# A fused gated-attention and MLP kernel on one core: a new order table of the same operations

## The chip, the cores and the metric

The kernel runs on one core of a Trainium2 chip. The metric is the device time of one execution in microseconds, the median of the runs. The engines of the core are TensorE (PE, with its weight loads as PEld), VectorE (DVE), ScalarE (ACT), GpSimd (POOL) and SyncE (SP, which here issues most of the DMAs).

## The reference

Per batch (4) and head (8), over 768 steps of width 48, a gated linear attention with a complex decay is computed; its real part goes through a layer norm, an MLP with a hidden width of 4 x 384, and a residual.

```python
mag = np.sqrt(a_re * a_re + a_im * a_im)
scale = np.minimum(mag, 0.999) / (mag + 1e-06)
a_re_n, a_im_n = (a_re * scale, a_im * scale)
for t in range(S):
    new_re = ar * S_re - ai * S_im
    new_im = ar * S_im + ai * S_re
    kv = np.einsum('bhd,bhe->bhde', k[:, :, t], v[:, :, t])
    S_re, S_im = (new_re + kv, new_im)
    y[:, :, t] = np.einsum('bhd,bhde->bhe', q[:, :, t], S_re)
...
xn = (x - mu) / np.sqrt(var + 1e-06) * g_ln
ch = np.maximum(xn @ w_ch1, 0.0) @ w_ch2
return (x + ch)
```

## The kernel before

The 4 x 768 steps are cut into 24 chunks n of 128 steps, two chunks making one of 12 pairs P (three pairs per batch). Every operation has a name: `kind.P.half.part` for work on a pair (pair 0 is cut into two halves of its heads, the others have half 0 alone), `kind.n` for work on a chunk, `mm1.P.group.part` and `mm2.n.part` for the MLP.

For a pair: `are` and `aim`, `q`, `k` and `vf` are the loads. ACT takes `ln` of a_re and its reciprocal `iv`; `r` = a_im/a_re, `r2` its square, `u` the log of 1 + r2, and DVE sums `l` and clamps it (`lc`): the log of the decay. A matmul with a triangular matrix (`dec`, L481) sums it along time, and ACT makes `e` and `en`, the exponential and its inverse. `th` is the arctangent of r, `ph` (L506, L514) sums it along time on PE with a carry `car` from the pair ahead, and `sin`, `cos` come from ACT (`abs` or the quarter turn `qt` prepares the cosine). `qe` and `ke` are q and k times the exponentials, `qs` and `ks` these times cosine and sine, stacked in one 128-row operand. `qs` and `ks` are transposed to `qsT` and `ksT`, by PE (`qT`, `kT`, L612) with a copy by ACT or DVE, or by a transposing DMA on SP (L617).

For a chunk: `am` (L635) is the 128 x 128 score of each head, `atm` its masked copy (DVE, PSUM to SBUF), `gm` (L663) and `G` the state that is carried on, `y` (L685, L688) the output, `x` its copy in SBUF, `bn` the statistics of the layer norm, `xtr` (L706) with `xT` the transposed x; `rstd` the inverse deviation. Per pair, `mm1` (L740, weights w1b, the gain and the mean folded in by `wp` and `wc`) makes the hidden layer in three groups, `relu` copies it (ACT or DVE), `mm2` (L772, weights w2b) is the second product, `oa` and `ot` scale it and add x, and `st` stores. `wl.0` to `wl.5` load the weights from POOL's own DMA queue; `warm` (L805) are matmuls without a use, put into PE's waits in the start; `tab` (L810) are loads of ACT's function table, one for logarithm and exponential and one for sine and arctangent.

What sets the order is a table written out in the code, `PLAN`. Each word is one operation: its name, the engine after the colon (P, A, V, G, S for PE, ACT, DVE, POOL, SP), the PSUM bank where it has one, and behind an @ another operation after whose last instruction it has to wait, although no data go between them. These waits are called turns: they keep a POOL operation behind a DVE operation, since the two engines share a port to SBUF. The words are emitted one after another, so each engine gets its instructions in the order of the table and runs them in that order. Tiles are rings of two to ten buffers (`RINGS`); an operation that writes a ring's buffer again has to stand behind the last reader of that buffer.

Of the kernel before, what the change touches and what calls it, by code (L numbers as in the profile page):

```python
# [39 lines left out]
aim.0.0:A are.0.0:S pickf:V tab.log.0:A ln.0.0:A iv.0.0:A are.1.0:S gln:S ue:G cmean:G uth:V r.0.0:V are.0.1:S one:G  # L40
r2.0.0:A u.0.0:A l.0.0:V ln.1.0:A aim.0.1:S ln.0.1:A q.0.1:S iv.0.1:A pick:G@r.0.0 lc.0.0:V warm.0:P0 warm.1:P0
warm.2:P0 warm.3:P0 warm.4:P0 warm.5:P0 warm.6:P0 warm.7:P0 warm.8:P0 warm.9:P0 warm.10:P0 warm.11:P0 warm.12:P0
warm.13:P0 warm.14:P0 warm.15:P0 warm.16:P0 warm.17:P0 warm.18:P0 warm.19:P0 warm.20:P0 warm.21:P0 warm.22:P0
# [4 lines left out]
warm.47:P0 warm.48:P0 warm.49:P0 warm.50:P0 warm.51:P0 warm.52:P0 warm.53:P0 dec.0.1:P2 aim.2.0:S en.0.0:A6 pad.qs.2:G
k.0.1:S wl.1:G@lc.1.0 en.0.1:A2 iv.2.0:A wl.0:G r.2.0:V warm.54:P0 warm.55:P0 warm.56:P0 warm.57:P0 warm.58:P0
warm.59:P0 warm.60:P0 dec.1.0:P4 e.1.0:A4 qrow:G@r.2.0 en.1.0:A4 k.0.0:S are.3.0:S pad.qs.1:G e.0.1:A2 r2.2.0:V  # L50
ke.0.0.0:V car0.0:G e.0.0:A6 qe.0.0.0:V u.2.0:A wgc:V warm.61:P0 warm.62:P0 warm.63:P0 warm.64:P0 warm.65:P0
# [18 lines left out]
ph.3.0:P0 atm.2:V4 car.3.0:V0 u.3.0:A xtr.3:P2 xT.3:V2 y.2:P6 x.2:A6 abs.3.0:V0 r.4.0:G mm1.0.2.0:P4 tab.trig.5:A  # L70
sin.3.0:A0 G.3:V7 xtr.2:P2 xT.2:V2 k.3.1:S are.6.0:S bn.2:V mm1.0.2.1:P4 mm1.1.1.0:P2 are.7.0:S mm1.1.2.1:P6
mm1.1.1.1:P2 bn.3:V cos.3.0:A relu.0.2:V4 bn.1:V pad.ks.2:G@ks.1.0.1 mm1.1.2.0:P6 relu.1.2:V6 mm1.1.0.1:P4 l.3.0:V
are.5.0:S ke.2.0.1:G@ks.1.0.1 ks.2.0.0:V th.4.0:A mm1.1.0.0:P4 mm2.0.0:P0 lc.3.0:V relu.1.1:A2 q.4.0:S qs.2.0.0:V
aim.6.0:S mm2.1.0:P3 mm2.1.1:P3 r2.4.0:G@ks.1.0.0 tab.log.6:A u.4.0:A ks.2.0.1:V vf.3.0:S aim.5.0:S relu.1.0:A4
# [137 lines left out]
def kernel(  # L212
# [13 lines left out]
    B, H, S, D = q.shape  # L226
# [615 lines left out]
```

## Time and profile before

| what | value |
|---|---|
| runs | 189.58, 189.34, 189.30 us; median 189.34 us |
| span of the profiled execution (first to last instruction) | 187.08 us, 2.26 us under the median of the runs |
| busy | PE 176.4, DVE 153.7, ACT 160.0, POOL 111.1 us |
| loads of ACT's table | 19, 24.4 us |
| HBM read, written | 28.31 MB, 4.72 MB |

The page gives a span for its execution, and no time of its own for it. Busy time of PE counts matmuls from issue to end, and consecutive ones overlap, so 176.4 us is more than the array needs. A row of the chain of waits or of the list in order of time begins with the start in us from the span's start and the duration in us. In the groups by line, the columns are line, engine, operation, tiles written and read with their shapes, count, busy us in all, mean ns of one, and the idle time ahead of them with what ended it.

### The profile page before, as it was taken

The page shows a single profiled execution, that of the slowest core. Times are in us where ns is not written, and L with a number is a line of the kernel's source. Part 1 is how long each engine was busy: PE and PEld are TensorE (multiplying, and loading weights), DVE is VectorE, ACT ScalarE, POOL GpSimd, SP SyncE. Part 2 cuts the span into 40 slices and gives each one's busy share as a digit, 9 for nine tenths or more (in the row PEclk, how much of TensorE's full clock was granted, in tenths as well). Part 3 has the DMA queues.
Part 4 walks back from the last instruction along what each step waited for, and adds up shares of the span by engine and source line. Part 5 has one row for each costly group of instructions (what it writes and reads, how often), then busy time and mean ns, then how long its engine had stood idle before and what let it go on. Part 6 is the DMA issues. An engine that isn't in the chain of part 4 may idle for free.

```text
span 187.1 us, 5110 instructions
## 1 busy us (share of the span) xinstructions
PE 176.4 (94%) x2025; PEld 135.1 (72%) x2027; DVE 153.7 (82%) x275; ACT 160.0 (86%) x228; POOL 111.1 (59%) x130
## 2 busy tenths in 40 slices
PE   5978898999999999999999999999999998999993
PEld 3756565787767789866687696878867866778772
DVE  1479999999989999999979989899879888866332
ACT  3889999999999989999999999998999897274560
POOL 3328699589207996288176692365879759420600
PEclk9999999999999999999999999999999999999999
DMA  5999999999999999699999997999999969996122
GB/s 148 291 256 227 223 260 189 207 206 194 233 261 239 219 221 191 128 203 309 204 155 238 256 265 92 185 247 169 216 175 215 203 144 229 210 199 173 40 90 84
DMA packets 132439, 37.39 MB, mean 200 GB/s; under 512 B 126528, under 2 KB 132416, under 8 KB 132416
## 3 DMA queue, kind: packets, MB, share of 16 engines
q1 hardware_dynamic: 123040, 32.45, 83.9%
q0 software_dynamic: 2784, 2.36, 8.2%
q10 hardware_dynamic: 6592, 2.26, 4.7%
q8 instruction: 16, 0.26, 0.6%
q14 instruction: 7, 0.06, 0.1%
HBM read 28.31 MB, written 4.72 MB: 177 GB/s over the span
## 4 chain that ended last, share of the span: by engine, by line
PE 71%; DVE 10%; DMA 6%; ACT 4%; POOL 3%; SPq 2%; issue 2%; DVEq 0%; POOLq 0%
PE banks L772 25%; PE banks L740 21%; PE banks L635 5%; PE banks L612 4%; PE banks L506 4%; PE banks L481 4%; DMA aim<-in_a_im_dram 3%; PE banks L685 2%; DMA qsT<-qs 2%; PE banks L706 2%; PE banks L688 2%; DMA are<-in_a_re_dram 2%; PE banks L663 2%; SPq L408 1%; DVE r L293 1%
## 5 line engine op out<-in xcount | busy, mean ns | idle before, releaser
L772 PE MATMUL banks<-w2b,h 128*128 128x384 bf16 (+1 forms) x300 | 53.8, 319 | 0.0
L740 PE MATMUL banks<-xT,w1b 128*128 128x256 bf16 x432 | 51.4, 272 | 0.2 <-DVE xT L290 0.2
L740 PEld LDWEIGHTS <-w1b 128*128 128x128 bf16 x432 | 41.3, 98 | 6.3 <-issue 0.4
L772 PEld LDWEIGHTS <-h 128*128 128x128 bf16 x300 | 27.1, 97 | 13.3
L293 DVE TENSOR_TENSOR atm<-banks,mask 128x1024 bf16<-128x1024 f32 x24 | 28.8, 1219 | 5.1 <-PE banks L635 5.0
L757 ACT ACTIVATE h<-banks 128x1024 bf16<-128x1024 f32 (+1 forms) x24 | 23.8, 1003 | 5.3 <-PE banks L740 5.1
L293 POOL TENSOR_TENSOR qe<-q,e 128x384 bf16<-128x384 f32 x19 | 17.5, 929 | 15.7 <-ACT e L485 9.1
L810 ACT ACT_TABLE_LOAD x19 | 24.4, 1283 | 1.7 <-PEq L826 1.3
L293 POOL TENSOR_TENSOR ke<-k,en 128x384 bf16<-128x384 f32 x16 | 14.8, 939 | 7.5 <-DVE qs L293 6.8
L759 DVE TENSOR_SCALAR h<-banks 128x1024 bf16<-128x1024 f32 (+1 forms) x13 | 15.2, 1169 | 3.6 <-PE banks L740 3.6
L805 PE MATMUL banks<-u_e 128*128 128x256 f16 x111 | 15.5, 297 | 2.2 <-POOL u_e L322 2.2
L635 PE MATMUL banks<-qsT,ksT 128*128 128x128 bf16 x192 | 14.1, 219 | 1.0 <-DMA qsT<-qs 0.7
L805 PEld LDWEIGHTS <-u_e 128*128 128x128 f16 x111 | 11.5, 106 | 4.5 <-POOL u_e L322 1.9
L293 POOL TENSOR_TENSOR r<-aim,are 128x768 f16<-128x768 f32 x7 | 12.6, 1811 | 3.0 <-ACT are L454 3.0
L635 PEld LDWEIGHTS <-ksT 128*128 128x128 bf16 x192 | 11.9, 98 | 2.5 <-issue 1.1
L293 POOL TENSOR_TENSOR qs<-qe,trig 128x768 bf16<-128x768 bf16 (+1 forms) x8 | 12.6, 1576 | 1.6 <-DVE qe L293 0.9
L470 DVE SCALAR_TENSOR_TENSOR l<-r,w 128x768 f16<-128x768 f16 (+1 forms) x13 | 12.3, 949 | 1.3 <-ACT r L466 1.1
L785 POOL TENSOR_TENSOR ot<-ot,x 128x384 f32<-128x384 f32 x11 | 10.5, 966 | 4.6 <-ACT ot L778 4.3
L698 DVE BATCH_NORM_STATS2 stats<-x 128x6 f32<-128x384 bf16 x24 | 13.1, 548 | 0.0
L288 ACT CAST x<-banks 128x384 bf16<-128x384 f32 x19 | 8.8, 478 | 5.0 <-PE banks L688 4.5
L293 POOL TENSOR_TENSOR ks<-ke,trig 128x768 bf16<-128x768 bf16 (+1 forms) x7 | 10.7, 1539 | 2.8 <-DVE qs L293 1.6
L685 PE MATMUL banks<-v,atm 128*128 128x48 bf16 x192 | 11.9, 183 | 0.0
(101 smaller groups left out, 380.4 us busy)
## 6 DMA issues: line engine op xcount, KB each, us to landing
q<-in_q_dram SPq DMA_DIRECT2D x24, 192.0 KB, 4.7
k<-in_k_dram SPq DMA_DIRECT2D x24, 192.0 KB, 4.5
are<-in_a_re_dram SPq DMA_DIRECT2D x11, 384.0 KB, 4.8
aim<-in_a_im_dram SPq DMA_DIRECT2D x11, 384.0 KB, 4.8
vf<-in_v_dram SPq DMA_DIRECT2D x19, 192.0 KB, 4.3
out_dram<-ot SPq DMA_DIRECT2D x18, 192.0 KB, 3.5
w1b<-in_moe_w_ch_dram POOLq DMA_DIRECT2D x3, 384.0 KB, 6.4
w2b<-in_moe_w_ch_dram POOLq DMA_DIRECT2D x3, 384.0 KB, 7.8
```

The source lines that it names most:

```text
L293: {"DVE": nc.vector, "POOL": nc.gpsimd}[eng(name)].tensor_tensor(**kw)
L470: nc.vector.scalar_tensor_tensor(out=S_("l"), in0=S_("r2"), scalar=0.5, in1=S_("w"), op0=ALU.mult, op1=ALU.add)
L635: nc.tensor.matmul(ps[:, h], lhsT=T("ksT", n)[:, h], rhs=T("qsT", n)[:, h], start=True, stop=True)
L685: nc.tensor.matmul(ps[:, h], lhsT=T("atm", n)[:, h], rhs=T("v", P)[:, c, h], start=True, stop=nfirst)
L698: nc.vector.bn_stats(out=T("stats", n), in_=T("x", n))
L740: nc.tensor.matmul(ps[:, jj], lhsT=w1b[:, dc, ts(gi * JG + jj, C)], rhs=T("xT", P)[:, dc].rearrange("p c t -> p (c t)"), start=(dc == 0), ...
L757: act(out=dst, in_=src, func=AF.Relu)
L759: nc.vector.tensor_scalar(out=dst, in0=src, scalar1=0.0, scalar2=None, op0=ALU.max)
L772: nc.tensor.matmul(bank(own)[:, 0:w], lhsT=T("h", P)[:, j, ts(c, C)], rhs=w2b[:, j, es], start=(j == 0), stop=(j == NJ - 1))
L785: nc.gpsimd.tensor_tensor(out=T("ot", n)[:, es], in0=T("ot", n)[:, es], in1=T("x", n)[:, es], op=ALU.add)
L805: g.add(f"warm.{i}", lambda i=i: nc.tensor.matmul(bank(f"warm.{i}")[:, 0:256], lhsT=u_e[:, 0, 0], rhs=u_e[:, 1].rearrange("p j t -> p (j t ...
L810: g.add(f"tab.{nm}.{i}", lambda tab=tab: nc.scalar.preload_act_table_set(tab))
```

## The change

`PLAN` is replaced by another table of the same operations; beside it, only the number of fillers that can be named is raised (111 to 200, of which the new table uses 103 where the old one used 111). Nothing of what an operation does is changed. The diff, of the table a line or two alone:

```diff
 PLAN = """
-aim.0.0:A are.0.0:S pickf:V tab.log.0:A ln.0.0:A iv.0.0:A are.1.0:S gln:S ue:G cmean:G uth:V r.0.0:V are.0.1:S one:G
...
+ue:G pad.qs.2:G car0.1:G are.0.0:S aim.0.0:S are.0.1:S tab.log.0:A car0.0:V are.1.0:S ln.0.0:A iv.0.0:A aim.0.1:S
...
-    for i in range(111):
+    for i in range(200):
         g.add(f"warm.{i}", lambda i=i: nc.tensor.matmul(
```

The table is two lines shorter, so every line number behind it is smaller by 2 in the new kernel. What the new table has otherwise than the old, counted by words (old, new):

| | old | new |
|---|---|---|
| turns (words with an @) | 49 | 35 |
| `warm` | 111 | 103 |
| `tab` | 19 | 18 |
| `qe` on POOL, on DVE | 19, 5 | 9, 15 |
| `ks` on POOL, on DVE | 7, 19 | 12, 14 |
| `r2` on ACT, POOL, DVE | 4, 4, 5 | 1, 7, 5 |
| `relu` on ACT, DVE | 24, 13 | 27, 10 |
| `v` on ACT, POOL, DVE | 2, 7, 3 | 4, 8, 0 |
| `vf` loads from ACT's queue, from SP's | 5, 19 | 0, 24 |
| `xT` by ACT, DVE, transposing DMA | 13, 10, 1 | 10, 12, 2 |

Three places show how the order moves. The first is DVE's queue at the end of the start, from the last products of the folded weights (L392, in the new kernel L390) to the masked scores and statistics of chunks 2, 3 and 0; the numbers in the names are buffers (atm2 is chunk 2's, sh1 is abs.3.0, car0 is written by car.3.0, xT1 by xT.3 and xT.2). Before:

```order
L392 SCALAR_TENSOR_TENSOR w1b_180<-w1b_180,gln_179,banks_63 128x512 x3
L293 TENSOR_TENSOR atm3_127<-banks_63,mask_174 128x1024
L290 CAST G2_130<-banks_63 128x384
L698 BN_STATS stats0_142<-x0_132 128x6
L699 BN_AGGR mv0_146<-stats0_142 128x2
L293 TENSOR_TENSOR atm2_126<-banks_63,mask_174 128x1024
L527 TENSOR_SCALAR car0_167<-banks_63 32x384
L290 COPY xT1_157<-banks_63 128x3x128
L551 TENSOR_REDUCE sh1_105<-banks_63 128x768
L293 TENSOR_TENSOR G3_131<-banks_63,dec1_95 128x384
L290 COPY xT1_157<-banks_63 128x3x128
```

Now:

```order
L390 SCALAR_TENSOR_TENSOR w1b_180<-w1b_180,gln_179,banks_63 128x512 x2
L291 TENSOR_TENSOR atm3_127<-banks_63,mask_174 128x1024
L390 SCALAR_TENSOR_TENSOR w1b_180<-w1b_180,gln_179,banks_63 128x512
L288 CAST G2_130<-banks_63 128x384
L291 TENSOR_TENSOR atm2_126<-banks_63,mask_174 128x1024
L696 BN_STATS stats0_142<-x0_132 128x6
L697 BN_AGGR mv0_146<-stats0_142 128x2
L549 TENSOR_REDUCE sh1_105<-banks_63 128x768
L288 COPY xT1_157<-banks_63 128x3x128 x2
L291 TENSOR_TENSOR G3_131<-banks_63,dec1_95 128x384
L525 TENSOR_SCALAR car0_167<-banks_63 32x384
```

The masked scores of chunk 2 (atm2) have moved ahead of chunk 0's statistics, one part of the folded weights behind atm3, and car0 and G3 behind both xT1 copies.

The second is SP's queue of loads in the start, behind the first loads of pair 0's k (k0_73); are0_64 is are.3.0, are1_65 is are.4.0, aim0_67 is aim.3.0, and q, k and vf carry their pair's number as the buffer's. Before:

```order
L449 DMA are0_64<-in_a_re_dram 128x8x96
L408 DMA k2_75<-in_k_dram 128x8x48
L408 DMA q1_71<-in_q_dram 128x8x48
L408 DMA q2_72<-in_q_dram 128x8x48
L408 DMA q1_71<-in_q_dram 128x8x48
L449 DMA are1_65<-in_a_re_dram 128x8x96
L408 DMA vf0_76<-in_v_dram 128x8x48
L408 DMA k1_74<-in_k_dram 128x8x48
L449 DMA aim0_67<-in_a_im_dram 128x8x96
L408 DMA k1_74<-in_k_dram 128x8x48
L408 DMA vf1_77<-in_v_dram 128x8x48
L408 DMA q2_72<-in_q_dram 128x8x48
```

Now:

```order
L370 DMA gln_179<-in_moe_g_ln_dram 128x3x1
L406 DMA q1_71<-in_q_dram 128x8x48 x2
L447 DMA are0_64<-in_a_re_dram 128x8x96
L406 DMA k1_74<-in_k_dram 128x8x48
L447 DMA aim0_67<-in_a_im_dram 128x8x96
L406 DMA vf0_76<-in_v_dram 128x8x48 x2
L406 DMA k1_74<-in_k_dram 128x8x48
L406 DMA q2_72<-in_q_dram 128x8x48
L406 DMA vf1_77<-in_v_dram 128x8x48 x2
L447 DMA are1_65<-in_a_re_dram 128x8x96
L406 DMA q2_72<-in_q_dram 128x8x48
L447 DMA aim1_68<-in_a_im_dram 128x8x96
```

The loads of q and k of pair 2 and of are.4.0 have moved behind those of k of pair 1, of aim.3.0 and of v of pair 0 (vf0); half of vf0 came from ACT's queue before and stands here now.

The third is SP's queue late in the program, at the transposes of chunks 20 and 21 (chunk 20 is buffer 0, chunk 21 buffer 1); xT1_157 is chunk 18's transposed x. Before:

```order
L712 DMA_TRANSPOSE xT1_157<-x8_140 128x3x128
L617 DMA_TRANSPOSE ksT1_117<-ks1_111 128x8x128
L408 DMA q2_72<-in_q_dram 128x8x48
L617 DMA_TRANSPOSE ksT0_116<-ks1_111 128x8x128
L617 DMA_TRANSPOSE qsT1_121<-qs1_114 128x8x128
L617 DMA_TRANSPOSE qsT0_120<-qs1_114 128x8x128
L408 DMA vf1_77<-in_v_dram 128x8x48 x2
```

Now:

```order
L710 DMA_TRANSPOSE xT1_157<-x8_140 128x3x128
L406 DMA q2_72<-in_q_dram 128x8x48
L406 DMA k2_75<-in_k_dram 128x8x48
L615 DMA_TRANSPOSE qsT1_121<-qs1_114 128x8x128
L615 DMA_TRANSPOSE ksT1_117<-ks1_111 128x8x128
L615 DMA_TRANSPOSE qsT0_120<-qs1_114 128x8x128
L615 DMA_TRANSPOSE ksT0_116<-ks1_111 128x8x128
L793 DMA out_0_dram<-ot4_166 128x384
```

The four transposes now stand in a row with the one for chunk 21's q first, its k second, and both loads of pair 11 ahead of them; a store follows where the loads of v did.

More of the change, by code (lines that the diff above doesn't have):

```diff
@@ L70 @@
[L70 to L74, printed above, removed]
```

195 lines of the change are left out of this document (99 added, 96 removed).

## The prediction

> **What bounds the kernel now.** The stretches come first: a table of busy time, cut at the two moments that the chain of waits marks (45.07, where it turns to matmuls, and 183.90, where the last matmul is over).
>
> ```profile
> core 0: us, PE busy (x) PEld busy (x) DVE busy (x) ACT busy (x) POOL busy (x), PEclk, DMA share, GB/s
> 7.86:45.07 37.21, 32.85 (x389) 25.02 (x391) 33.55 (x62) 35.76 (x52) 27.30 (x39) 1.00 1.16 226
> 45.07:183.90 138.83, 137.92 (x1604) 105.94 (x1603) 117.76 (x207) 119.90 (x171) 80.50 (x78) 1.00 0.95 195
> 183.90:187.08 3.18, 0.00 (x0) 0.00 (x0) 0.42 (x1) 0.00 (x0) 0.00 (x0) 1.00 0.28 90
> ```
>
> From 45.07 to 183.90 TensorE is busy 137.92 of 138.83 us at the full granted clock (1.00), while DVE is at 85% and ACT at 86%. A busy PE is not a PE at its peak, so the next view is its rows in order of time: in the chain of waits they follow each other at the rate of their size.
>
> ```profile
> 45.07 4.09 PE banks L740 x36
> 80.20 2.60 PE banks L772 x16
> 164.12 0.34 PE banks L706 x6
> 154.88 4.00 DMA qsT<-qs
> 179.96 3.94 PE banks L772 x36
> 183.93 0.42 DVE ot L788
> ```
>
> 36 matmuls of 256 columns in 4.09 us are 0.11 us each, 16 of 384 columns in 2.60 us are 0.16 us each. From 45.07 on nothing but such rows stands in the chain, apart from one piece around 154.88. So the kernel is three pieces: a filling of 45.07 us, 138.8 us of matmuls end to end, and 3.2 us behind the last of them (one DVE operation and the last store). An operation that goes from one other engine to another inside the middle piece is worth nothing unless a matmul waits for it. What can move the end: the moment at which the dense piece starts, the holes in it, and its amount of matmuls.
>
> **The dense piece starts when DVE lets it.** DVE in order of time, then ACT and PE at that place:
>
> ```profile
> 40.56 0.55 DVE L698 BATCH_NORM_STATS2 stats<-x 128x6 f32<-128x384 bf16 x1
> 41.15 0.18 DVE L699 BATCH_NORM_AGGREGATE mv<-stats 128x2 f32<-128x6 f32 x1
> 41.25 1.19 DVE L293 TENSOR_TENSOR atm<-banks,mask 128x1024 bf16<-128x1024 f32 x1
> 42.47 0.56 DVE L527 TENSOR_SCALAR car<-banks 32x384 f16<-32x384 int16 x1
> 43.07 0.36 DVE L290 COPY xT<-banks 128x384 bf16<-128x384 bf16 x1
> 43.34 0.95 DVE L551 TENSOR_REDUCE sh<-banks 128x768 f16<-128x768 int16 x1
> 44.21 0.55 DVE L293 TENSOR_TENSOR G<-banks,dec 128x384 bf16<-128x384 f32 x1
> 44.67 0.35 DVE L290 COPY xT<-banks 128x384 bf16<-128x384 bf16 x1
> 43.33 0.48 ACT L288 CAST x<-banks 128x384 bf16<-128x384 f32 x1
> 43.86 0.34 PE L706 MATMUL banks<-ident,x 128*128 128x128 bf16 x3
> 45.07 1.14 PE L740 MATMUL banks<-xT,w1b 128*128 128x256 bf16 x9 [0.21 <-DVE xT L290]
> ```
>
> The row at 45.07 is the first matmul of pair 1's hidden layer, and it waits for the second xT copy (44.67, chunk 2). That copy's input, the transpose at 43.86, was over at 44.20; the copy came 0.5 us later because abs (43.34) and G.3 (44.21) stood ahead of it.
>
> **Change, part 1: the start.** The operations of PE ahead of that matmul are the same ones in both tables, in another order, so the moment can be compared directly. In the new DVE order atm.2 stands ahead of chunk 0's statistics, and car.3.0 and G.3 stand behind the two xT copies. By start-to-start spacings of the rows: old, from 40.56: statistics 0.69, atm 1.22, car 0.60, xT.3 0.27, abs 0.87, G.3 0.46, xT.2 0.35, which ends at 45.02. New, from the same moment: atm.2 1.22, statistics 0.69, abs 0.87, xT.3 0.27, xT.2 0.35, which ends at 43.96. The difference is car and G.3: 0.60 + 0.46 = **1.06 us**. PE and ACT allow it: atm.2 would end 0.69 earlier, so y.2, x.2 and the transpose (1.42 us from atm's end at 42.44 to the transpose's start at 43.86) are ready from 43.17, ahead of where DVE would take the copy. What becomes late next is G.3, which feeds G's chain and no matmul of the next microseconds (gm.4 stands 16 us of PE work further on in the new order), and car.3.0, read by the phase of pair 4, 13 us on.
>
> Upstream of 40.56 more moves. Two half-width squares go from ACT to DVE, where a full-width product of 2-byte operands takes 0.55 us (the ks row of part 3), and the exponentials of half 0 are taken ahead of ln.2.0. The load queue is put in the order of need:
>
> ```profile
> 13.33 3.67 SPq L408 DMA_DIRECT2D q<-in_q_dram  x3
> 17.10 4.20 SPq L449 DMA_DIRECT2D are<-in_a_re_dram  x1
> 21.34 1.44 SPq L408 DMA_DIRECT2D vf<-in_v_dram  x1
> 22.82 0.77 SPq L408 DMA_DIRECT2D k<-in_k_dram  x1
> ```
>
> In the old table one are load holds the SP queue for 4.20 us (others take about 1), and v and k of the first pairs stand behind it. In the new one, q.2 and k.2 and that are load go behind k.1, aim.3 and vf.0. DVE had no long idle from 20 to 40 in the old run (9.52 and 9.44 busy of 10, below), so earlier data can bring only what DVE is relieved of; and the products of the first pairs that change between DVE and POOL nearly cancel (two qe and the two squares come to DVE, two ke, one qs and one ks leave it).
>
> ```profile
> 20.00:30.00 10.00, 9.07 (x90) 5.79 (x90) 9.52 (x20) 9.57 (x16) 8.51 (x11) 1.00 1.15 236
> 30.00:40.00 10.00, 9.06 (x136) 7.59 (x136) 9.44 (x15) 9.89 (x13) 8.12 (x9) 1.00 1.09 201
> ```
>
> DVE's idle in these 20 us is 1.04 us in all: the gain upstream is at most that, and at worst a loss of the same size (a new wait where an idle one was). I take 0.2 us of gain, since DVE gets no more work there than it loses and its inputs come earlier. Start: **-1.26 us**, between -2.1 and 0.
>
> **Part 2: the hole.** In the dense piece, the one wait of PE that the table of waits shows is for a transposing DMA:
>
> ```profile
> 151.31 1.23 SPq L617 DMA_TRANSPOSE ksT<-ks  x1
> 152.60 0.57 SPq L408 DMA_DIRECT2D q<-in_q_dram  x1
> 153.27 1.43 SPq L617 DMA_TRANSPOSE ksT<-ks  x1
> 154.88 3.19 SPq L617 DMA_TRANSPOSE qsT<-qs  x2
> 159.01 0.61 PE L635 MATMUL banks<-qsT,ksT 128*128 128x128 bf16 x8 [0.71 <-DMA qsT<-qs]
> ```
>
> am.21 waits 0.71 us for qsT.21, third in a row of four transposes. In the new order qsT.21 is the first of the four and ksT.21 the second, with two small loads ahead of both; that takes one transpose issue (1.43) and its spacing off am.21's wait and adds one load (0.57): about 0.9 us earlier, enough for 0.71. What is late next: am.20, which needs the fourth transpose; in the new PE order a block of mm2.19 (0.65) lies between the two. I take -0.5 of the 0.71 (0 to -0.71).
>
> **Part 3: amounts.** xtr.22 leaves PE (chunk 22 goes through a DMA transpose instead): three transposes, half of the six in 0.34 us, **-0.17 us**. It costs if the transposed x.22 comes later than mm1.11; it is put behind two stores on SP, with some 4 us of PE work between y.22 and mm1.11 as cover. Another table load goes from ACT, and products change between DVE and POOL:
>
> ```profile
> L810 ACT ACT_TABLE_LOAD x19 | 24.4, 1283 | 1.7 <-PEq L826 1.3
> L293 POOL TENSOR_TENSOR qe<-q,e 128x384 bf16<-128x384 f32 x19 | 17.5, 929 | 15.7 <-ACT e L485 9.1 <-DVE r L293 4.1 <-DVE qs L293 1.4
> L293 POOL TENSOR_TENSOR ks<-ke,trig 128x768 bf16<-128x768 bf16 x6 | 9.7, 1636 | 2.7 <-DVE qs L293 1.6 <-DVE ke L293 1.0
> L293 DVE TENSOR_TENSOR qe<-q,e 128x384 bf16<-128x384 f32 x5 | 2.7, 554 | 0.8 <-ACT e L485 0.8
> L293 DVE TENSOR_TENSOR ks<-ke,trig 128x768 bf16<-128x768 bf16 x16 | 8.6, 550 | 0.2
> ```
>
> The table load (1.28 us) is the last one, at a place where the matmuls hide ACT; ten qe go to DVE (+5.5 us there, -9.3 on POOL), five ks to POOL (-2.8 and +8.2). Three relus and three v copies leave DVE as well, so that neither DVE nor ACT ends with more work than before. All this lies beside 138.8 us of matmuls: 0, and with that cover gone it would show as the port rival below. Eight fillers fewer of 0.11 us each fill waits in the start: 0. The small other holes of the dense piece (0.91 - 0.71 = 0.2 us by the busy sum) I leave as they are. The tail has the same form, one DVE operation and a store: 0.
>
> Sum: -1.26 - 0.5 - 0.17 = **-1.9 us**: a span of 187.08 - 1.9 = 185.2. The median of the runs, 189.34, lies 2.26 above the span; with that kept, **187.4 us**.
>
> **Rivals.**
> 1. *The port takes it back (slower).* An unguarded POOL operation beside a DVE one holds it up:
>
> ```profile
> 17.70 0.91 POOL L293 TENSOR_TENSOR qe<-q,e 128x384 bf16<-128x384 f32 x1 [0.56 <-ACT r L466]
> 17.82 1.20 DVE L293 TENSOR_TENSOR ke<-k,en 128x384 bf16<-128x384 f32 x1
> ```
>
> The ke product took 1.20 us where its like took 0.55, and ended 0.41 us after POOL's end, so it stood still meanwhile: 0.65 us. The new table has 35 turns (waits that keep POOL behind a DVE operation) where the old has 49, and puts more of the long ks (1.64 us) on POOL; a DVE product that starts just behind a ks could stand up to 1.6 us. It decides where DVE feeds a matmul at once. From three such places of 0.65 us the gain is gone; with five the kernel is at 187.4 + 3.2 = 190.6 us. For it: fewer turns, more POOL work. Against it: DVE's 21 us of idle in the dense piece, and less DVE work. The Trainium skill (SBUF — State Buffer, Who interferes with whom) says that the pair of ports is an exclusive lock and that the second to start is blocked wholly; the two rows agree with it. By that rule alone, with every lost turn (14) costing DVE as in that row, 9 us would be added to DVE, still inside its 21 us of idle.
> 2. *No gain at the start (about the same).* Another input sets 45.07: the new order needs v, k, xT and weights in other places, and a weight load at a bad moment stops SP as the 4.20 us row does. Then only 0.17 and part of the hole remain: 189.1 us, and with a wait of 0.3 us more, no change.
> 3. *The upstream gain arrives too (faster).* -2.1 at the start, all of 0.71, 0.17 and 0.2 of the small holes: 186.2 us.
> 4. *The change is in name only:* the table load and the fillers are gone by count (19 to 18, 111 to 103), but neither is on the path, and were the order neutral elsewhere, 189.2. It is part of case 2.
>
> **How the numbers follow.** My forecast (186.7 to 188.5) 0.54; case 3 0.14; cases 2 and 4 0.15 (0.09 within 0.2%, 0.05 faster, 0.01 slower); case 1 0.17. The range reaches from case 3's 186.2, a little lower for its own spread, to near the middle of case 1: 186.0 to 190.0. The smallest change that can be told here is about 0.2%, 0.4 us. Faster: 0.54 + 0.14 + 0.05 = 0.73; within 0.2%: 0.09; slower: 0.17 + 0.01 = 0.18.
>
> **What would show it.** In the changed profile the first matmul of pair 1's hidden layer starts near 43.8; PE has no wait for a transposing DMA near 157; the last matmul ends near 182.0; the dense piece is 138.1 us long. Part 1 is wrong if that matmul starts after 44.7, part 2 if PE still waits over 0.5 us for ksT or qsT. The port rival shows as DVE products of 0.9 us and more where 0.55 is normal, with PE waits for DVE behind them. A dense piece longer than 140 us would make the prediction wrong whatever the start does.

## The result, and the profile after

After: 196.47 us, median of 4 runs (195.79 to 198.06); before, in the same session, 189.46 (189.30 to 190.81). Ratio 1.034, 95% interval 1.027 to 1.041: the new order is **slower by 3.4%**, 7.0 us, where 1.9 us of gain was forecast. Some executions fall into a slower state, and every ratio here is of the others alone, while the medians are of all (sp_later, fill, back6, y18, p1 and actq_late below have one or two slow ones).

The profiled execution has a span of 195.9 us (before 187.1); it is the slowest of the four, with a mean granted clock of 0.983, where the fastest, 195.79 us, had 1.000 and the other two 0.991. The table of busy time, cut as in the prediction (first decay matmul, first matmul of pair 1's hidden layer, end of the last matmul):

```profile
core 0: us, PE busy (x) PEld busy (x) DVE busy (x) ACT busy (x) POOL busy (x), PEclk, DMA share, GB/s
8.96:47.46 38.50, 34.25 (x383) 25.68 (x385) 33.00 (x59) 33.16 (x49) 22.98 (x28) 0.91 1.06 208
47.46:192.72 145.26, 138.56 (x1603) 105.50 (x1600) 120.45 (x212) 121.94 (x166) 85.94 (x82) 1.00 0.93 187
```

The start is 47.46 and not 45.07 (+2.4), the middle piece 145.26 and not 138.83 (+6.4), with nearly the same busy time of TensorE in it (138.56, before 137.92): mostly holes, then (6.7 us, before 0.9). The tail (192.72 to 195.90) is the same 3.18. And a column that was 1.00 throughout before: the granted clock of the start is 0.91.

**The start.** The changed kernel's rows in order of time (start, duration, engine; in brackets the idle time before and what ended it):

```profile
20.07 2.03 DVE L377 TENSOR_SCALAR gc<-cmean,gln 128x128 bf16<-128x128 f32 x3
...
20.24 1.78 POOL L291 TENSOR_TENSOR qs<-qe,trig 128x384 bf16<-128x384 bf16 x2 [0.87 <-ACT trig L530]
...
22.16 0.39 PE L386 MATMUL banks<-w1b,gc 128*128 128x512 bf16 x1 [1.35 <-DVE gc L377]
```

wgc, three small operations on DVE, takes 2.03 us beside two POOL products that nothing holds back (qs.0.0.1, qs.0.1.1); wp.1 on TensorE waits 1.35 us for it, and the carry car.0.1 behind it on DVE holds the next matmul for 0.74 us. TensorE is then sparsely busy, and this follows (busy time by stretch, the granted clock third from the end):

```profile
20.00:23.00 3.00, 0.98 (x4) 0.40 (x5) 2.94 (x7) 1.77 (x4) 1.78 (x2) 0.94 1.23 232
23.00:26.00 3.00, 2.72 (x10) 0.97 (x10) 2.97 (x7) 0.86 (x2) 1.04 (x2) 0.50 0.86 202
26.00:29.00 3.00, 3.00 (x12) 1.67 (x11) 0.95 (x2) 2.97 (x4) 3.00 (x4) 0.50 1.00 194
```

TensorE was busy for 0.98 of 3.00 us, and for the next six it was granted half its clock: 10 and 12 matmuls where the rows of before have 24 and 37. The Trainium skill (TensorE: Matmul & The Clock Gate, Part 1: The HAM clock gate) says that the clock halves after an idle window of about 3.4 us and that the windows run free of the program; the trace agrees with the halving, though TensorE was sparse there and not idle.

**The middle piece.** What TensorE waits for in it, from the table of waits (window 47.46 to 193):

```profile
PE banks L633 <- DMA ksT<-ks: 2.0, 1, 2.0
PE banks L479 <- DVE h L757: 1.6, 1, 1.6
PE banks L738 <- DVE qsT L288: 0.9, 1, 0.9
PE banks L633 <- DMA qsT<-qs: 0.8, 1, 0.8
```

With three smaller ones (0.6 for ACT's e, 0.3 for the transposing DMA of an xT, 0.2 for DVE's atm) these make 6.4 us, 3.1 of it for transposing DMAs. The same table of before, from 45.07 to 184, has 0.7 us for such a DMA and 0.2 for DVE. Two of the holes show what is new. At l.3.0 (behind it on DVE stands relu.1.2, which frees the bank of the matmuls dec.3.0):

```profile
49.49 0.80 POOL L368 DMA_DIRECT2D w2b<-in_moe_w_ch_dram  x1
49.64 2.43 DVE L468 SCALAR_TENSOR_TENSOR l<-r,w 128x768 f16<-128x768 f16 x1
50.32 0.93 POOL L291 TENSOR_TENSOR ke<-k,en 128x384 bf16<-128x384 f32 x1
...
54.46 0.81 PE L479 MATMUL banks<-l,u_e 128*128 128x384 f16 x4 [1.61 <-DVE h L757]
```

l.3.0 took 2.43 us (0.95 in before): it stood through POOL's descriptor writing for wl.5 and through the product behind it. The largest hole is at am.20 (chunk 20's scores), 1.97 us at 170.16. The chain of waits leads there:

```profile
147.03 2.65 DMA out_dram<-ot
149.78 0.62 DVE ot L786
...
152.79 1.64 POOL qs L291
154.43 1.43 issue
155.90 0.91 POOL ke L291
156.89 3.56 POOL ks L291 x2
...
163.94 1.33 SPq L615
165.31 4.80 DMA ksT<-ks
170.16 0.62 PE banks L633 x8
```

It runs through SP's queue, through a store on which DVE's ot.15 waits, through POOL's products and into the fourth of four transposing DMAs. (The 1.43 us of "issue" ahead of ke.10.0.1 end as its load k.10.1, issued at 152.66, lands at 155.83.) And SP itself had stopped long before. Its longest wait but the one for the last outputs, from the table of waits:

```profile
SPq L615 <- POOL ks L291: 8.0, 1, 8.0
```

8.0 us in one piece, 71 to 79, ahead of the transposing DMA ksT.8, whose input ks.4.0.1 had moved to POOL. No load left in that time.

### The profile page after: what moved, and what is told of

The parts are those of the page before. It is cut to its first block, busy times and chain, and to the rows that moved or that the text cites. A ratio compares the mean times of both kernels' runs of the same rounds, so it can differ in the third digit from the quotient of the medians.

```text
span 195.9 us, 5097 instructions
## 1 busy us (share of the span) xinstructions
PE 177.9 (91%) x2014; PEld 135.0 (69%) x2016; DVE 156.3 (80%) x277; ACT 160.3 (82%) x221; POOL 115.3 (59%) x133
## 4 chain that ended last, share of the span: by engine, by line
PE 32%; DVE 24%; DMA 11%; SPq 11%; ACT 8%; issue 6%; POOL 6%; POOLq 0%; DVEq 0%; ACTq 0%
PE banks L738 10%; PE banks L770 9%; SPq L406 5%; DMA out_dram<-ot 4%; DVE atm L291 4%; DVE l L468 3%; DMA aim<-in_a_im_dram 3%; SPq L447 3%; SPq L615 3%; PE banks L504 2%; DMA ksT<-ks 2%; DMA are<-in_a_re_dram 2%; DVE h L757 2%; PE banks L633 2%; POOL ks L291 2%
## 5 line engine op out<-in xcount | busy, mean ns | idle before, releaser
L770 PE MATMUL banks<-w2b,h 128*128 128x384 bf16 (+1 forms) x300 | 54.5, 319 | 0.0
L755 ACT ACTIVATE h<-banks 128x1024 bf16<-128x1024 f32 (+1 forms) x27 | 26.7, 1005 | 6.7 <-PE banks L738 6.5
L291 POOL TENSOR_TENSOR ks<-ke,trig 128x768 bf16<-128x768 bf16 (+1 forms) x12 | 18.4, 1545 | 4.4 <-DVE ks L291 2.9
L291 POOL TENSOR_TENSOR qs<-qe,trig 128x768 bf16<-128x768 bf16 (+1 forms) x9 | 13.2, 1476 | 7.3 <-DVE qe L291 4.1
L416 POOL TENSOR_SCALAR v<-vf 128x768 bf16<-128x768 f32 x8 | 7.2, 899 | 17.0 <-DVE qsT L288 7.7
L291 POOL TENSOR_TENSOR r<-aim,are 128x768 f16<-128x768 f32 x6 | 11.2, 1866 | 6.7 <-ACT are L452 6.7
L468 DVE SCALAR_TENSOR_TENSOR l<-r,w 128x768 f16<-128x768 f16 (+1 forms) x13 | 13.4, 1030 | 1.6 <-ACT r L464 1.6
L757 DVE TENSOR_SCALAR h<-banks 128x1024 bf16<-128x1024 f32 (+1 forms) x10 | 11.6, 1158 | 3.1 <-PE banks L738 3.1
L479 PE MATMUL banks<-l,u_e 128*128 128x384 f16 (+1 forms) x52 | 10.6, 328 | 3.4 <-DVE l L471 1.7
L450 ACT ACTIVATE w<-are 128x768 f32<-128x768 f32 (+1 forms) x13 | 10.3, 794 | 3.7 <-DMA are<-in_a_re_dram 3.7
## 6 DMA issues: line engine op xcount, KB each, us to landing
q<-in_q_dram SPq DMA_DIRECT2D x24, 192.0 KB, 3.9
k<-in_k_dram SPq DMA_DIRECT2D x24, 192.0 KB, 3.9
vf<-in_v_dram SPq DMA_DIRECT2D x24, 192.0 KB, 4.2
out_dram<-ot SPq DMA_DIRECT2D x18, 192.0 KB, 3.3
```

The source lines that it names most:

```text
L291: {"DVE": nc.vector, "POOL": nc.gpsimd}[eng(name)].tensor_tensor(**kw)
L468: nc.vector.scalar_tensor_tensor(out=S_("l"), in0=S_("r2"), scalar=0.5, in1=S_("w"), op0=ALU.mult, op1=ALU.add)
L479: nc.tensor.matmul(heads(ps[:, c]), lhsT=u_e[:, c, j], rhs=step(T("l", P), j), start=(j == 0), stop=(j == R - 1))
L755: act(out=dst, in_=src, func=AF.Relu)
L757: nc.vector.tensor_scalar(out=dst, in0=src, scalar1=0.0, scalar2=None, op0=ALU.max)
L770: nc.tensor.matmul(bank(own)[:, 0:w], lhsT=T("h", P)[:, j, ts(c, C)], rhs=w2b[:, j, es], start=(j == 0), stop=(j == NJ - 1))
```

## The experiments

Theories from these two profiles: **port** (POOL beside DVE: wgc, l.3.0), **clock** (half speed at 23 to 30 us), **stop** (SP's 8 us ahead of ksT.8 make everything after it late), **queue** (SP has too much to issue: 144 operations, 137 in the old table), **order behind 118 us** (chains of the new order itself). "Start" below is the first matmul of pair 1's hidden layer in the profile of that run. "Landing" is the last completion of the last input load (of k, q or vf of pair 11) in its trace. Each ratio is to before as it ran beside that run (its median was then 189.8 to 190.2). Before, as profiled: start 45.07, landing 162.1, span 187.1; after: 47.46, 172.1, 195.9.

| run | median us | ratio to before (95%) | start | landing | span |
|---|---|---|---|---|---|
| oldstart | 195.18 | 1.027 (1.022 to 1.031) | 46.54 | 169.6 | 193.4 |
| newstart | 192.23 | 1.009 (1.005 to 1.013) | 45.35 | 166.2 | 191.0 |
| sp_later | 197.08 | 1.027 (1.019 to 1.036) | 45.83 | 169.8 | 194.8 |
| turn_wgc | 192.42 | 1.012 (1.005 to 1.018) | 43.74 | 166.8 | 189.3 |
| fill | 196.24 | 1.032 (1.023 to 1.041) | 44.64 | 168.2 | 191.8 |
| turn2 | 193.28 | 1.014 (1.006 to 1.022) | 43.45 | 167.5 | 191.8 |
| best1 | 193.88 | 1.018 (1.010 to 1.026) | 45.33 | 169.6 | 192.8 |
| best2 | 192.65 | 1.012 (1.004 to 1.020) | 43.60 | 167.1 | 192.0 |
| k10 | 193.18 | 1.016 (1.012 to 1.020) | 43.70 | 167.5 | 191.6 |
| k10b | 193.19 | 1.018 (1.011 to 1.024) | 43.24 | 166.9 | 191.6 |
| join3 | 194.56 | 1.020 (1.013 to 1.027) | 44.04 | 167.0 | 193.0 |
| back6 | 195.00 | 1.024 (1.019 to 1.029) | 46.11 | 167.8 | 191.7 |
| y18 | 194.99 | 1.028 (1.022 to 1.034) | 43.66 | 166.1 | 192.8 |
| late | 192.99 | 1.017 (1.011 to 1.023) | 43.57 | 167.7 | 191.5 |
| p1 | 192.20 | 1.012 (1.006 to 1.018) | 46.0 | 165.0 | 189.8 |
| p12 | 192.63 | 1.017 (1.013 to 1.022) | 46.0 | 164.7 | 190.1 |
| actq | 192.35 | 1.013 (1.008 to 1.019) | 43.45 | 166.9 | 190.5 |
| actq_late | 192.68 | 1.017 (1.009 to 1.026) | 43.51 | 167.1 | 190.8 |

**1. Start and rest apart.** Two kernels join the tables at mm1.1.1.0; what the first part has issued is left out of the second.

```diff
  oldstart
+ the old table up to mm1.1.1.0
+ the changed table, without the operations above
  newstart
+ the changed table up to mm1.1.1.0
+ the old table, without the operations above
```

> The old table up to pair 1's hidden layer (mm1.1.1.0), and from there the new table's order of what is left. Start and dense piece are independent (my theory: 2.4 us lost in the start, about 6.5 us in holes of the dense piece): mm1.1.1.0 near 45.1 us, SP again stopped some 8 us ahead of ksT.8, time 193.5 to 195.0. Rival (the holes come from loads that the new start sends late): the holes go with the start, 188.5 to 190.5.

> The new table up to mm1.1.1.0, and from there the old table's order. If start and dense piece are independent: mm1.1.1.0 near 47.4, no stop of SP of 8 us near 71, time 191.0 to 192.5. Rival (holes come from late loads of the start): above 194. Rival (the old rest has slack for the start's lateness): below 190.5.

oldstart is 2.7% above before, so most of the loss stands behind the start. It is not split cleanly: this old start came at 46.54 (POOL's qe waited 3.00 us for a DVE product, and TensorE 1.64 us for a POOL fill behind it, of which the profile of before has 1.37 and nothing). The three other profiles that have the old start, back6, p1 and p12, show the same: a wait of POOL's qe of 2.9 to 3.0 us, one of TensorE for the fill of 1.3 to 1.6, a start at 46.0 to 46.1. So the 45.07 that the prediction counted from is at the early end of a spread of over 1 us. And newstart's new start, with the same slow wgc, came at 45.35 and not 47.46. What differs most is the clock, as the same three stretches of newstart show:

```profile
20.00:23.00 3.00, 1.48 (x5) 0.40 (x5) 2.97 (x6) 1.67 (x4) 1.78 (x2) 1.00 1.24 240
23.00:26.00 3.00, 2.82 (x20) 1.69 (x20) 2.97 (x8) 1.91 (x3) 1.14 (x2) 1.00 0.95 218
```

TensorE is sparsely busy here too (1.48 of the 3 us, 0.98 in after), and the clock stays at 1.00. That the halving differs from execution to execution, the four of after say themselves (mean granted clock 0.983 to 1.000); the two profiled starts lie 2.1 us apart.

**2. The wait for wgc, and the clock.** One word for the port; for the clock, work for TensorE where it was idle:

```diff
  turn_wgc
- qs.0.0.1:G
+ qs.0.0.1:G@wgc
  fill
  ph.0.1:P4
+ warm.120:P0 ... warm.127:P0
...
  wp.1:P1
+ warm.128:P0 ... warm.133:P0
```

> The changed kernel with one word more: POOL's qs.0.0.1 waits for wgc. Port theory: the three operations of wgc take 0.7 us again and not 2.03, wp.1 ends 1.3 us earlier, mm1.1.1.0 comes 1.0 to 2.4 us earlier (the higher end if PE, less sparsely busy, keeps its full clock at 23.7 to 29.8), time 194.0 to 195.4. Rival (the start is lost to the halved clock, which stays as PE is still sparse, or to wl.0's late issue): mm1.1.1.0 within 0.5 us of 47.4 and 195.8 to 196.8.

> The changed kernel with 14 more fillers on TensorE, 8 behind ph.0.1 and 6 behind wp.1, where it was idle; wgc stays beside POOL. Clock theory (TensorE too sparsely busy from 19.3 to 23.7 us is given half speed for some 6 us): the granted clock stays at 1.00 through 23 to 30 us in every execution, mm1.1.1.0 comes between 44.3 and 45.0, time 193.0 to 194.8. Rival (the clock falls whatever TensorE does, or only the wait for wgc costs): mm1.1.1.0 past 46.5 and 195.8 to 198.

turn_wgc, the same rows as above (timeline):

```profile
19.72 0.68 DVE L377 TENSOR_SCALAR gc<-cmean,gln 128x128 bf16<-128x128 f32 x3
...
20.54 2.23 POOL L291 TENSOR_TENSOR qs<-qe,trig 128x384 bf16<-128x384 bf16 x2 [1.52 <-DVE gc L377]
```

wgc takes 0.68 us again, the granted clock is 0.997 or more in all four executions, and the start is at **43.74, where the prediction had put it (43.8)**. Of 3.4% loss, 1.2% is left: one missing turn cost about 4 us (2.4 to 6 by the two intervals), more than the port theory expected (194.0 to 195.4) and more than wgc's wait of 1.35 us; how the rest of it comes about is open. Part 1 can now be compared with the forecast. The copy xT.2 in turn_wgc:

```profile
43.33 0.36 DVE L288 COPY xT<-banks 128x384 bf16<-128x384 bf16 x1 [0.37 <-PE banks L704]
```

From the first moved operation (the forecast's 40.56, here 39.93) to the start it took 3.81 us, before 4.51: the moves gave 0.70 and not 1.06, since the copy waited 0.37 for TensorE's transpose, and all that stands ahead of them gave 0.63 and not 0.2. So the sum was met, its two terms were not.

With fill the clock held too (0.997 or more in four executions, start 44.64 with wgc still slow). Yet only the profiled execution gained (194.02); the others took 196.0 and more at the same full clock, and no profile shows them. The clock explains the late start of the profile of after; of its time it can hardly explain more than the 2.3 us that lie between the execution at full clock (195.79) and the profiled one (198.06). Nor does the turn make sure of the clock: best1 (experiment 4) has it and wgc at 0.68 us, and fell all the same, its start at 45.33:

```profile
20.00:23.00 3.00, 1.67 (x10) 0.61 (x9) 2.92 (x7) 1.73 (x4) 2.10 (x2) 0.94 1.24 228
23.00:26.00 3.00, 3.00 (x12) 1.35 (x10) 3.00 (x7) 1.65 (x3) 1.95 (x3) 0.50 0.61 146
```

Over the 20 profiles the clock fell in the start in three, with TensorE busy 0.98 (after), 1.30 (sp_later) and 1.67 (best1) of the 3 us from 20 to 23. It stayed at 1.00 in newstart with 1.48, in oldstart, p1, p12 and back6 with 1.36 to 1.66 from 23 to 26, and wherever TensorE had 2.0 or more in both stretches: no fall without a sparse stretch, but a sparse stretch is not enough.

**3. SP's stop.**

```diff
  sp_later, SP's order
- k.6.1 ksT.8 k.6.0 are.8.0 st.0 qsT.9 q.5.0 vf.5.1 q.5.1
+ k.6.1 k.6.0 are.8.0 st.0 q.5.0 vf.5.1 q.5.1 ksT.8 qsT.9
```

> The changed kernel with ksT.8 and qsT.9 moved on SP alone, behind the loads k.6.0, are.8.0, q.5.0, vf.5.1, q.5.1 and the store st.0. Queue-stop theory: the loads run while ks.4.0.1 is still on POOL, the stretch near 71 to 79 us is no longer at 3 GB/s, and of the holes behind 120 us (4.5 us) most go: 190.5 to 193.0. Rival (SP's queue is simply too full since all vf loads stand on it, or DMA is saturated whatever the order): 195.0 to 196.8, with the holes at 126, 155 and 170 still there.

No gain that can be told (1.027 against 1.034). The loads did overtake ksT.8: k.6.0 was issued at 68.8 and not 80.5. But the stop came again behind them, when SP had nothing else whose buffer was free:

```profile
70.00:85.00 15.00, 14.93 (x171) 12.17 (x170) 14.39 (x28) 14.07 (x19) 9.55 (x7) 1.00 0.64 135
85.00:150.00 65.00, 64.08 (x752) 48.65 (x750) 59.52 (x106) 62.05 (x86) 36.97 (x39) 1.00 0.99 206
```

The DMA share of 70 to 85 is 0.64 (after 0.45, before 0.88; the figures of these two stand at the end of this section), and behind it 0.99, where after has 1.09 and before 1.07. The gap was moved, not closed; the theory is neither shown nor refuted by it.

**4. l.3.0, and five places of TensorE's order,** on top of turn_wgc:

```diff
  turn2, POOL's order
- wl.5 ke.2.0.0 ke.2.0.1@l.3.0
+ ke.2.0.0@l.3.0 ke.2.0.1@l.3.0 wl.5
  best1 = turn2 and, on TensorE
+ mm2.9.1 ahead of kT.13, mm2.16.1 ahead of am.19, mm2.17.2 ahead of mm1.9.1.1
+ mm2.19.2 and mm2.18.0 ahead of am.20, mm2.11.0 ahead of am.13
  best2 = best1 and sp_later's move
```

> turn_wgc, and on POOL wl.5 behind ke.2.0.1 and ke.2.0.0 waiting for l.3.0. Port theory: l.3.0 takes 0.95 us and not 2.43, dec.3.0 comes 1.5 to 1.8 us earlier, and the end with it: 190.4 to 191.2. Rival (the later stops, of transposing DMAs above all, are set by SP and DMA and not by TensorE's position, and take it back): 191.8 to 192.6, with the holes at am.19, mm1.9.1.1 and am.20 longer by as much together.

> turn2, and on TensorE alone five places in which other work is put ahead of a waiting operation: mm2.9.1 ahead of kT.13, mm2.16.1 ahead of am.19, mm2.17.2 ahead of mm1.9.1.1, mm2.19.2 and mm2.18.0 ahead of am.20, mm2.11.0 ahead of am.13. If the rest of the loss is these places' own (the new order put a waiting operation too early): 0.75 + 0.73 + 0.55 + 0.57 + 0.35 = 2.95 us less than turn2, 187.3 to 188.7. Rival (who waits for these operations is late then, and the holes come again behind them): within 0.8 us of turn2.

> best1, and ksT.8 and qsT.9 behind the loads and the store on SP as in sp_later. Queue-stop theory, which sp_later spoke against: 0.8 us or more below best1, since SP no longer runs late behind 80 us. Rival (loads and transposes have slack enough of it): within 0.5 us of best1.

turn2, in order of time and then in the table of waits of TensorE:

```profile
45.63 0.95 DVE L468 SCALAR_TENSOR_TENSOR l<-r,w 128x768 f16<-128x768 f16 x1
```

```profile
PE banks L633 <- DMA ksT<-ks: 2.0, 1, 2.0
```

The hole of 1.6 us at dec.3.0 is gone and the time is the same (1.014, turn_wgc 1.012): am.20, which waited 0.41 us in turn_wgc, waits 2.0 us again, and am.19 1.1 us. (Of turn_wgc the fastest of four executions was profiled, of turn2 the slowest; the medians, 192.42 and 193.28, say that nothing was gained.) The time is the rival's. It was so for best1 and best2 too: work put ahead of the waiting matmuls, and the time stays.

**5. The chain ahead of am.20.**

```diff
  k10 = turn2, SP's order
- ksT.18 st.10 qsT.18 vf.9.0 ksT.19 qsT.19 k.10.1
+ k.10.1 ksT.18 st.10 qsT.18 vf.9.0 ksT.19 qsT.19
  k10b = k10, POOL's order
- qs.10.0.0@qe.10.0.1 ke.10.0.1@qe.10.0.1 ks.10.0.0@atm.18 ks.10.0.1@atm.19
+ ke.10.0.1@qe.10.0.1 ks.10.0.0@atm.18 ks.10.0.1 qs.10.0.0
  y18 = turn2; TensorE, ACT, SP
- am.19 mm2.16.1 gm.18 y.18         x.18:V         xT.18 q.11.1 k.11.0
+ mm2.16.1 gm.18 y.18 am.19         x.18:A         q.11.1 k.11.0 xT.18
  late = k10b and y18, ke.10.0.1 and ks.10.0.0 without turns
```

> turn2 with one load moved on SP: k.10.1 ahead of ksT.18, st.10, qsT.18, vf.9.0, ksT.19 and qsT.19. In turn2 POOL waited 1.8 us for it ahead of ke.10.0.1, and behind that stand ks.10.0.0 and ks.10.0.1 (end 155.5 us, before 149.1), which the four transposes ahead of am.20 wait for. Queue-order theory (the new order puts this load behind stores and transposes that stop SP): that wait goes, am.20 comes 1.2 to 2 us earlier, 191.2 to 192.2. Rival (SP, which is issuing 18 of every 20 us, only moves the loss to what the load has overtaken): within 0.5 us of turn2, with a longer stop at am.19.

> k10, and on POOL ke.10.0.1, ks.10.0.0 and ks.10.0.1 ahead of qs.10.0.0, the last two of these without their turns except that of ks.10.0.0 behind atm.18. Theory (POOL's order and its turns make ks.10.0.1 late): it ends 2.5 to 4 us earlier than in turn2, am.20 does not wait over 0.6 us, 190.0 to 191.5. Rival (qs.10.0.0 is then the last input of the transposes, or SP is late anyway): within 0.5 us of k10.

> turn2, and around 150 us: on TensorE mm2.16.1, gm.18 and y.18 ahead of am.19, x.18 back on ACT (behind th.11.0), and on SP q.11.1 and k.11.0 ahead of xT.18. Chain theory (am.19's wait for qsT.19 holds y.18, that x.18, that xT.18 on SP, and that the four transposes of am.20): xT.18 is issued 1 to 1.5 us earlier, qsT.21 and its three followers 1.3 to 1.6 us, am.20 near 163.7, 191.3 to 192.3. Rival (SP or DMA is simply late there): qsT.21 moves by less than 0.6 us and the time stays within 0.5 us of turn2 (193.3).

> y18 together with k10b, and ke.10.0.1 and ks.10.0.0 on POOL without their turns. If chain and POOL's order bind by turns (each was hidden behind the other when it was mended alone): qsT.21 near 153.5, am.20 no longer waits over 0.6 us, 189.5 to 191.0. Rival (limit of SP and DMA): 192 and more. Port rival (ks without its turn holds relu or qe on DVE): DVE's products near 147 us take over 0.9 us, and 191.5 to 193.

In k10 ke.10.0.1 no longer waits for its load, but ks.10.0.1 ends at 155.3 (turn2 155.5), am.20 still waits 1.46 us (turn2 1.95) and am.18 and am.19 wait 1.4 together. In k10b ks.10.0.1 ends only 1.2 us earlier than in turn2, where 2.5 to 4 were expected, and am.20 waits 1.60. In late it ends at 151.2 and am.20 no longer waits; 1.31 us stand at mm1.9.1.1 and 1.04 at a matmul of mm2 instead. None was faster than turn2. y18 was worse: am.20's wait is 0.2 us there, but TensorE waited 1.78 us for xT.18 at 157.97, and the clock was 0.50 from 158.0 to 161.4 (0.76 over 158 to 165); the mean granted clock was 0.98 to 0.99 in all four executions.

**6. Queue.** Eight loads and stores that the old table had on ACT's queue go back there.

```diff
  actq = turn2, actq_late = late
- vf.5.0:S vf.6.1:S st.2:S st.1:S vf.7.0:S st.8:S vf.9.1:S st.9:S
+ vf.5.0:A vf.6.1:A st.2:A st.1:A vf.7.0:A st.8:A vf.9.1:A st.9:A
```

> turn2, with vf.5.0, vf.6.1, st.2, st.1, vf.7.0, st.8, vf.9.1 and st.9 issued by ACT instead of SP, as in the old table, at the places in ACT's order where they stood in time; all else as in turn2. SP theory (SP issues 17 to 18.5 of every 20 us from 80 on, and each thing it does late makes the transposes late): SP runs 3 to 6 us earlier by 145 us, the holes at am.19 and am.20 (1.3 and 2.1 us in turn2) lose most of themselves, 190.0 to 191.8. Rival (DMA itself or the compute engines' chains set the transposes): within 0.6 us of turn2 (193.3), SP idle instead. Rival (ACT pays for the issues): 193.5 to 194.5.

> late, with the same eight on ACT's queue. If SP's fullness and the chains of late bind by turns: 188.5 to 190.3, xT.18 issued before 153 us and no wait over 0.6 us behind 140. Rival (neither binds): within 0.6 us of late (193.0).

The same times as turn2 and late. SP was relieved of eight issues and reached xT.18 at 152.32, where turn2 reached it at 152.17. So the count of SP's operations is not the limit. From 85 to 153 us its table of waits has, in both runs, many short waits (2.7 us at most) for DVE, TensorE, POOL and ACT, and 0.6 us in one of them for a DMA.

**7. Joins further on.**

```diff
  join3
+ turn2's table up to mm1.3.0.0, then the old table
  back6
+ the old table up to mm1.6.0.0, then the changed table
```

> turn2's order up to mm1.3.0.0 (near 76 us), and from there the old table's order of what is left. If the new start is a gain once POOL stands aside for wgc and l.3.0, and what loses stands behind 76 us: mm1.1.1.0 near 43.5, and the end 0.5 to 1.3 us below before, a ratio of 0.993 to 0.998. Rival (loads and stores sent by the old rest find the seam's queue late, as in newstart, which stopped 1.9 us at mm2.0.2): 1 to 2 us above before.

> The old table up to mm1.6.0.0 (near 118 us), and from there the changed kernel's order. If the dense piece's loss stands behind 118 us (am.19, mm1.9.1.1, am.20: SP's order of loads, stores and transposes, POOL's ks.10.0.1): am.20 waits 1 to 2 us again, 2.0 to 4.0 us above before. Rival (those stops only show the lateness that the queue brought from ahead of 118 us): within 1.0 us of before.

back6 has none of the new order ahead of 118 us and loses 2.4%, with am.20 waiting as before:

```profile
165.36 0.34 PE L635 MATMUL banks<-qsT,ksT 128*128 128x128 bf16 x3 [1.88 <-DMA ksT<-ks]
```

Part of the loss therefore belongs to the late part by itself, as far as the seam allows to say (0.65 us of hole stand near it). join3's seam cost more than it could tell: 3.2 us of hole ahead of dec.5.0.

**8. The prediction's parts 1 and 2 in the old order.**

```diff
  p1, DVE's order
- bn.0 atm.2 car.3.0 xT.3 abs.3.0 G.3 xT.2
+ atm.2 bn.0 xT.3 abs.3.0 xT.2 car.3.0 G.3
  p12 = p1 and, on TensorE
- am.21 mm2.19.0
+ mm2.19.0 am.21
```

> The old order with the prediction's part 1 alone: on DVE, atm.2 ahead of bn.0, and car.3.0 and G.3 behind xT.2. Prediction's theory: mm1.1.1.0 comes 1.06 us earlier (near 44.0) and the end with it, a ratio of 0.994 to 0.996. Rival (the dense piece's later stops are set by SP's queue and do not move with the start): the matmul comes 1 us earlier and the end within 0.3 us of before, ratio 0.998 to 1.001, with am.21 waiting for longer.

> p1, and on TensorE mm2.19.0 ahead of am.21, whose wait of 0.71 us it then covers. Prediction's theory: 0.5 to 0.65 us below p1, ratio 0.991 to 0.994. Rival (the wait comes again behind it, at am.20 or gm.20): same as p1 within 0.2 us.

Both came out above before, by 1.2 and 1.7%. My edit had a wait of its own: car.3.0 now stands behind sin.3.0 of ACT, which reads the same bank, and G.3 behind it frees the bank that pair 1's third matmul group wants.

```profile
47.32 0.56 DVE L527 TENSOR_SCALAR car<-banks 32x384 f16<-32x384 int16 x1 [1.36 <-ACT trig L532]
```

TensorE waited 1.64 us for G.3. Their late start is not all of the edit's making: atm.3, ahead of everything that was moved, stands at 40.32 in p1 and at 38.97 in before, as in the other profiles with the old start. As a test of part 1 the run is spoilt; it gives one thing: against atm.3, xT.2 came only 0.42 us earlier than in before (5.28 behind atm.3's start, before 5.70), since x.2, which waits for y.2 in TensorE's order, did not move.

**What the runs say together.** No run beat before, and those with the best starts (43.2 to 43.8) all end between 189.3 and 192.8, p1 with a start at 46.0 at 189.8. Over the 20 profiles the span goes with the start hardly at all (correlation 0.33) and with the landing of the last input load closely (0.88): span less landing is 24.4 us, standard deviation 1.0. That says when, not why: a last load can be late because it was issued late. When the DMAs did their work is read from the DMA share. Before:

```profile
0.00:45.00 45.00, 38.46 (x421) 29.16 (x424) 35.42 (x68) 40.00 (x58) 30.49 (x53) 1.00 1.10 222
45.00:70.00 25.00, 24.79 (x304) 18.81 (x304) 23.75 (x44) 24.11 (x35) 15.58 (x15) 1.00 1.04 231
70.00:85.00 15.00, 15.00 (x160) 11.95 (x156) 14.45 (x26) 14.82 (x22) 9.15 (x9) 1.00 0.88 182
85.00:150.00 65.00, 64.96 (x783) 49.70 (x781) 58.03 (x103) 61.52 (x86) 42.08 (x41) 1.00 1.07 208
```

After:

```profile
0.00:45.00 45.00, 36.85 (x370) 27.33 (x373) 33.45 (x61) 35.92 (x52) 27.21 (x51) 0.92 1.00 211
45.00:70.00 25.00, 23.39 (x289) 18.13 (x287) 24.20 (x44) 23.49 (x35) 16.38 (x13) 1.00 1.06 207
70.00:85.00 15.00, 14.93 (x177) 12.08 (x175) 14.52 (x26) 14.52 (x19) 9.62 (x8) 1.00 0.45 103
85.00:150.00 65.00, 63.16 (x740) 47.27 (x739) 58.01 (x104) 60.43 (x84) 36.93 (x39) 1.00 1.09 212
```

From 85 to 150 us the share (the packets' time; it goes over 1) is 1.07 and 1.09, and none of the 20 profiles has more than 1.09 there. That is no ceiling, though: over shorter stretches the share is higher, here in turn_wgc and in before:

```profile
94.00:109.00 15.00, 14.41 (x170) 10.81 (x168) 13.24 (x21) 14.87 (x20) 9.88 (x10) 1.00 1.25 237
123.00:138.00 15.00, 14.96 (x189) 11.63 (x187) 12.95 (x23) 14.23 (x21) 12.07 (x11) 1.00 1.18 205
```

So it is not shown that the DMAs could not have made up for a gap. What the changed kernel loses earlier is (1.10 - 1.00) x 45 = 4.5 in the start and (0.88 - 0.45) x 15 = 6.5 around SP's stop; the other two stretches give back 0.5 and 1.3. That leaves 9.2 of DMA busy time, at a share of 1.06 some 8.7 us; the last load lands 9.9 us later (172.1, before 162.1), and the span is 8.8 longer. That the sum fits is close to bookkeeping: the DMA busy time up to the last load is nearly the same in all 20 profiles (167 to 172 us; before 1.05 x 162.1 = 170, after 0.99 x 172.1 = 170), so a later landing has to show as a lower share somewhere. It tells where the DMAs fell behind, not what held them. And no run closed the gap at 70 to 85 us and left the rest. best2 filled it (0.97) and had 1.01 behind it, with the same end: that speaks against the gap as the cause by itself.

## Why the prediction was wrong

- **The step that failed: the overlap in the middle piece.** "All this lies beside 138.8 us of matmuls: 0." TensorE was busy 99% of that piece in before, so everything beside it was taken as hidden, and of its waits only the one at am.21 was followed. The piece was to be 138.1 us and is 145.26. Of the 6.4 us by which it is longer than in before, 5.8 are holes (6.7, before 0.9): TensorE waits 3.1 us for transposing DMAs, 2.7 for DVE and 0.6 for ACT. The new order moved products between DVE and POOL, turns and SP's queue, and with them what these matmuls wait for.
- **A sign of it was in the profile.** The prediction reads the chain of before as "nothing but such rows" from 45.07 on, "apart from one piece around 154.88". That piece is 6.1 us long, from 152.74 to 158.88, through DVE, POOL and a DMA, and there is another of 1.4 us on DVE:

```profile
60.35 0.70 DVE qsT L290
...
152.74 0.36 DVE xT L290
```

- **Whether the DMAs are a second limit** (their share, 0.95, stood in the row that was quoted) stays open. SP's queue was read for the start and for the four transposes, not for its 8 us stop.
- **Part 1, the start (-1.26): wrong as made, and right in sum by luck once it was let through.** 43.8 was forecast; as made it is 47.46. With one turn added 43.74 was measured, made up of 0.70 and 0.63 instead of 1.06 and 0.2, against a profile of before whose start is itself at the early end of its spread. Upstream of 40.56 it was costed at 0.2 of gain and at worst at 1.04 of loss, the idle time of DVE. The loss there was wgc beside two POOL products (1.35 more) and the halved clock behind it. And the gain of 1.3 us in the start, where it came, did not reach the end.
- **Part 2, the hole at am.21 (-0.5): moved on.** TensorE no longer waits for qsT.21; am.20, named as "what is late next" with 0.65 us of cover, waits 1.97 us for the fourth transpose, which the new order makes later by all that stands ahead of it.
- **Part 3, xtr.22 (-0.17):** beside the rest not to be told. Five more ks on POOL, named there, include ks.4.0.1, which stopped SP.
- **The port rival (0.17)** named the mechanism of the start and of l.3.0, at 0.65 us a place. Two places had 1.36 (2.03 less 0.67) and 1.48 (2.43 less 0.95): an operation stood through two of POOL's, not one. Only the first showed in the time.
- **What would show it** held: start past 44.7, a wait of over 0.5 us for ksT, a middle piece longer than 140 us.

Shown: the missing turn at wgc (about 4 us of the 7), and that nine tenths of the time added to the middle piece are waits of TensorE. Shown within a seam: that the order behind 118 us loses by itself. Only argued: that the rest is DMA time lost at 70 to 85 us; best2 speaks against it. Left open: what is left of the loss, some 2 to 3 us, why fill's unprofiled executions were slow, and whether the changed order with wgc's turn and ks.4.0.1 back on DVE would reach before; that wasn't tried.

## What to carry to other kernels

An engine that is busy 99% of a stretch is not its only limit: an order that is changed around it can open holes in it. Before putting what lies beside it at nothing, read the DMA share beside its busy time, and ask of each moved operation which DMA waits for it in its queue, and what stands behind that DMA. When a mended wait comes back at another place with the time unchanged, mending waits one by one has stopped paying: look for what they have in common (which here was not found). And a turn that guards a few small operations which feed a matmul early on (wgc, 0.68 us) was worth several microseconds here.

## What the runs showed of the hardware

- The granted clock fell to 0.50 for some 6 us after 3 us in which TensorE was busy for 0.98 us, for 3.4 us behind a wait of 1.78 us (y18, 158.0 to 161.4) and for some 3.3 us behind one of 3.16 us (join3, 81.0 to 84.3). With 1.48 of 3 us busy and the same slow wgc it did not fall (newstart); with 1.67 it did (best1).
- A DVE operation beside POOL was held through two POOL instructions in a row, one of them a descriptor writing (l.3.0, 2.43 us for 0.95; 0.80 and 0.93 us on POOL). The Trainium skill (SBUF — State Buffer, Who interferes with whom) calls the shared ports an exclusive lock on which the second to start blocks for the whole instruction; the trace has it standing for more than one.
- Taking eight of SP's issues away changed nothing in when SP got through (xT.18 at 152.32, with them 152.17).
